# Weight and query loads issued at counted matrix instructions, in a kernel of a delta rule followed by a feed-forward block

## The chip, the cores and the metric

The kernel runs on one core of a Trainium2 chip. The metric is the device time of one execution in microseconds (us). A core has TensorE (PE in the profile, with its weight loads as PEld), VectorE (DVE), ScalarE (ACT), GpSimd (POOL) and SyncE (SP), each with its own queue of instructions in program order. Here SP only issues DMA transfers; they run on 16 shared DMA engines. The same engines also bring in the engines' own code.

## The reference

For each of 4 x 8 heads, over 768 tokens of 48 numbers, a state matrix is carried along by the delta rule; the result, seen as 3072 tokens of 384 numbers, goes through a feed-forward block.

```python
k_n = k / (norm(k) + 1e-6)
for t in range(S):
    y[t] = q[t] @ state
    state = state + beta[t] * outer(k_n[t], v[t] - state.T @ k_n[t])
x = y.transpose(0, 2, 1, 3).reshape(3072, 384)
h = x @ w_in                     # 384 x 2048, 64-bit input
out = (h * sigmoid(h)) @ w_out   # 2048 x 384, 64-bit input
```

## The kernel before

**Tiling.** The 768 tokens are worked through in 6 chunks of 128 (index c), each in two halves of 64 tokens. Inside a chunk the delta rule is solved with triangular matrices: scores of keys with keys and with queries (`score`, L517), the inverse of small 32 x 32 blocks on VectorE (`invert_first` for chunk 0, L653 to L684; `invert` for the others, L606), the joining of the blocks into 64 x 64 (`joins(0)` and `joins(1)`, whose products are L705, L721, L734 and L794), and the state's products (`keys`, `inner`, `old`, `new`, `update`). The score blocks go out to DRAM and come back in another layout (`block_out`, L564; `block_in`, L570). The feed-forward block takes each half's outputs through `hidden` (L1029, products with `w_in`, then Silu on ScalarE) and through `project` (L1064) or `combine` (L1136), which multiply with `w_out`.

**Weights.** The 64-bit weights are loaded in 16 pieces of 768 KB each, 8 of `w_in` (`fetch_w_in(i)`, L283) and 8 of `w_out` (`fetch_w_out(i)`, L295), and each is made 32-bit by `narrow`: two instructions on ScalarE (L224, L225), two on VectorE (L229, L233), one on GpSimd (L237). Pieces land in rooms that something else uses later: `raw` (a pool of three buffers shared with `gT`), `w_outs`, `spare` (in `sums_of_g`), `sums_of_w`.

**Order.** The order on each engine is written out by hand: `pin` chains every instruction behind the one before it on its engine. Every transfer of SP goes through `in_line`, which chains it behind the last transfer; if `pace` holds an instruction, the transfer also waits for that instruction to finish. `linked(fetch, ...)` puts the last transfer into `pace`, so that the next load waits until the one before it has landed. A string of words drives the long first part from L1496 on: `s` one step of solving chunk 0, `f` one step of narrowing, `r` one half of a `hidden` or `project` step, `j` one product of `joins(1)`, `q` one transpose of chunk 1's queries, `l` the lengths of chunk 1's keys, `b` the first two narrowing instructions of the next piece, `W7`, `w2` and `w3` the loads of those pieces, `v` the values of chunk 1. Loops from L1499 on do the same for chunks 1 to 5.

**Around the change.** `busy(n)` (L336) runs n products of `ident` with a state that is still zero, whose result nothing reads. During the 17 steps of `invert_first` the loop at L1330 runs seven of them, each behind a step of the inversion, and four transposes of chunk 1's keys (`turn`, L488). Ahead of that, SP's queue holds in this order: the four block stores of chunk 0 (four more go through ScalarE's queue), `block_in(0)`, `fetch_w_in(0)`, `load_k(1)`, `fetch_w_in(1)`, `load_v(0)`, and then:

```python
linked(fetch_w_in, 2)
linked(load_q, 1)
fetch_w_in(3)
linked(fetch_w_in, 4)
linked(fetch_w_in, 5)
linked(fetch_w_in, 6)
```

Later `W7`, `w2` and `w3` follow out of the string of words, and `fill` issues `w_out` pieces 0, 1 and 4 to 7 as soon as the narrowing of an earlier piece has freed their rooms. An fp32 product is four PE instructions (two weight loads and two products), a transpose two.

Of the kernel before, what the change touches and what calls it, by code (L numbers as in the profile page):

```python
# [11 lines left out]
U32 = mybir.dt.uint32  # L12
# [7 lines left out]
def kernel(  # L20
# [52 lines left out]
            mybir.DependencyInfo(how, mybir.DependencyReason.DATA), reason="order",  # L73
        )

    pins = {}

    def pin(op):

        engine = op.ins.engine  # L80
        if engine in pins:
            behind(op, pins[engine])
        pins[engine] = op
        return op

    line, pace = [], []
# [17 lines left out]
    def go(steps, n=1):  # L104
        for _ in range(n):
            next(steps, None)

    def together(*parts):
        for _ in zip_longest(*parts):
            pass  # L110
# [52 lines left out]
    def in_blocks(c):  # L163

        return 1 < c < NCH
# [3 lines left out]
    def linked(fetch, *args):  # L169

        pace.append(line[-1])
        fetch(*args)

    def load_k(c, bs=ALL):
# [98 lines left out]

    def fetch_w_in(i):
        if i in (0, 1, 6):
            raw = mlp.tile([P, SIZE], U32, name="raw", tag="gT", bufs=3)[:]
        elif i < 6:
            raw = room(i // 2 - 1, i % 2)
        else:
            raw = spare  # L280
        raw = raw.rearrange("p (a f) -> p a f", a=NKT)
        src = moe_w_in.rearrange("(a p) f -> p a f", p=P)[:, :, i * WF : (i + 1) * WF].bitcast(U32)
        in_line(nc.sync.dma_start(out=raw, in_=src))  # L283
        raws["in", i] = raw.rearrange("p a (f j) -> p a f j", j=2)
# [47 lines left out]
    def busy(n=1, after=None, how=NoSync):  # L332

        for _ in range(n):
            pw = bank(CC, "pw")
            done = pin(nc.tensor.matmul(  # L336
                pw[:, 0:DM], lhsT=ident[:],
                rhs=states[0][:].rearrange("p u a w -> p (u a w)")[:, 0:DM], start=True, stop=True,
            ))
            if after is not None:  # L340
                behind(done, after, how)
                after = None
# [138 lines left out]
    def turn(c, b, j, room, by_vector=False):  # L481

        if j == 0:
            kq_room(c, b)
        src, kq = (kbufs[c % 2], queries[c] if c < 2 else None)[j][:, b], kqs[c, b]
        pt = bank(room, "pt")
        for p in range(NP):
            pin(nc.tensor.transpose(  # L488
                pt[:, p * C : (p + 1) * C], src[:, p].rearrange("p e w -> p (e w)"), ident[:]
            ))  # L490
        ptv = pt[:].rearrange("p (a t) -> p a t", a=NP)
        if j == 1:
            if by_vector:
                pin(nc.vector.tensor_scalar(
                    out=kq[:, :, j, :], in0=ptv, scalar1=-1.0, scalar2=None, op0=ALU.mult
                ))
            else:
                pin(nc.scalar.mul(kq[:, :, j, :], ptv, -1.0))
        elif by_vector:
            pin(nc.vector.tensor_copy(out=kq[:, :, j, :], in_=ptv))  # L500
        else:
            pin(nc.scalar.copy(kq[:, :, j, :], ptv))
# [65 lines left out]
    def block_in(c):  # L568
        there, g, _ = blocks[c]
        in_line(nc.sync.dma_start(out=g, in_=there[:]))  # L570
# [716 lines left out]
    def first_queries(b):  # L1287
# [4 lines left out]
        turn(0, b, 1, M)  # L1292
        score(0, b, (1,), (A, CC), evacuate)

    block_in(0)
    busy(4)
    for _ in norm_steps(0):
# [4 lines left out]
    for t in xis:  # L1302
        pin(nc.gpsimd.memset(t, 0.0))
    step = block_steps(0)
    fetch_w_in(0)
    load_k(1)
    fetch_w_in(1)
    load_v(0)
    for c in range(1, NCH):
        beta_of(c)  # L1310
# [1 line left out]
    for b in range(2, B):  # L1312
        first_queries(b)
        busy(1)
    linked(fetch_w_in, 2)
    linked(load_q, 1)
    fetch_w_in(3)
    linked(fetch_w_in, 4)
    linked(fetch_w_in, 5)
    linked(fetch_w_in, 6)  # L1320
    begin(("in", 0))
    inv = invert_first(step)

# [5 lines left out]

    for n in range(1 + Q):  # L1330
        done = next(inv)
        if n in (4, 6, 8, 9, 11, 13, 15):
            busy(1, done, Sync)
        if n in (10, 12, 14, 15):
            turn(1, (10, 12, 14, 15).index(n), 0, M)
    corner, turned, straight = next(inv)
    pin(nc.gpsimd.memset(slab, 0.0))

    def joins(hf, between=()):

        for stage in (
            corner(0, hf), corner(1, hf), turned(0, hf), turned(1, hf), straight(0, hf), merge_half(0, hf, False),
            straight(1, hf), merge_half(1, hf, False), merge_half(0, hf, True), merge_half(1, hf, True),
        ):
            yield from stage
            for what in between[:1]:
                what()
            between = between[1:]

    def filled(n):  # L1350
        return lambda: fill(n)
# [5 lines left out]
    def none():  # L1357
        pass

    together(joins(0, [sized, none, none, filled(2), filled(1), none, none, filled(2), begin_next, none]))  # L1360
    masks(1, 0)
    masks(1, 1)

# [6 lines left out]
    def run(n=1):  # L1370

        for _ in range(n):
            name = next(needed, None)
            if name is not None:
                until(name)
            go(pieces)
            begin_soon()
# [62 lines left out]
    sizes_1 = [0, 1]  # L1440
    sums_made = sum_w()
    later = {}

    def script(text):

        nonlocal pieces
        for word in text.split():
            what, n = word[0], int(word[1:] or 1)
            if what == "s":
                go(solving, n)  # L1450
            elif what == "f":
                fill(n)
                begin_soon()
            elif what == "r":
                run(n)
            elif what == "e":
                eager.append(True)
            elif what == "l":
                go(long, n)
            elif what == "j":  # L1460
                go(rest, n)
            elif what == "q":
                turn(1, queries_1.pop(0), 1, M)
            elif what == "b":
                begin_next()
            elif what == "p":
                go(ready, n)
            elif what == "w":
                fetch_w_out(n)
            elif what == "W":  # L1470
                fetch_w_in(n)
            elif what == "h":
                size_half(1, pins[seen_on])
            elif what == "v":
                load_v(1)
            elif what == "k":
                load_k(2)
            elif what == "g":
                step = block_steps(1)
                pin(nc.gpsimd.memset(spread[:], 0.0))  # L1480
                later["inv"] = invert(1, step)
            elif what == "i":
                go(later["inv"], n)
            elif what == "z":
                size(1, sizes_1.pop(0))
            elif what == "t":
                until(("out", NWI - 1))
                go(sums_made, n)
            elif what == "m":
                go(long_2, n)  # L1490
            elif what == "c":
                run(999)
                pieces = chained(feed_forward(1, 0), feed_forward(1, 1))

    for text in (
        "s f3 s q s q b j20 j8 r j16 f j16 q f j20 r j4 f j32 j8 b j4 q j4 W7 r f r j16 j6 f j4 j8 f j8 f b j8 f j4 j8 r j12 e r f j99 h w2 f r l f s f l r2 w3 l p r l f p l s l f r l r l3 p l s l3 p l2 r l f l4 f l f l3 p l s l2 s2 f r v f r p l3 g i p f l p f i p f l i r3 i r i2 r3 i2 r i r i3 b r2 f2 r3 i r i2 r2 i f b i4 f r f r2 f r3 f i2 r f i f r3 f r f i f r i2 r i2 k i2 b r2 i r i r z r i r s r b z s b r2 t r2 f s r2 t2 m2 t2 b m f r m s f b r m r m2 b m f s r s m4 c s m7 r t s m r m5 s r m m t t",  # L1496
    ):
        script(text)
    for c in range(1, NCH):  # L1499
        if c > 1:  # L1500
            solving = solve(c)
            for n in range(9):
                go(solving)
                run((2, 2, 2, 2, 1, 1, 2, 2, 2)[n])
                if n == 5:
                    pieces = chained(pieces, feed_forward(c, 0), feed_forward(c, 1))
        assert next(solving, 0) == 0
        go(long_2, 99)
        if c + 1 < NCH:
            ready = prepare(c + 1)  # L1510
            go(ready)
            run(2)
            step = block_steps(c + 1)
            for _ in ready:
                run(2)
            run(6)
            for n, _ in enumerate(invert(c + 1, step)):
                run(int(n % 4 != 3 and n != 24))
                if n == 3:
                    load_k(c + 2)  # L1520
                    if in_blocks(c + 2):
                        load_blocks(k, c + 2, ALL)
            after = lengths(c + 2) if c + 2 < NCH else iter(())
            for _ in range(8 if c == 1 else 10):
                run()
                go(after, 4)
            go(after, 99)
    run(999)


# [28 lines left out]
```

## Time and profile before

| what | value |
|---|---|
| three runs | 650.11, 657.17, 660.95 us; median 657.17 |
| the profiled execution | 652.37 us, with a span of 650.4 us from first to last instruction |
| busy share of the span | PE 96%, DVE 61%, ACT 33%, POOL 14% |
| granted clock of TensorE | 0.99 on average; 0.51 from 40 to 50 us |
| DMA | 54.70 MB, mean 84 GB/s |
| PE busy, 20 to 70 us | 41.7 of 50 us |
| PE busy, 200 to 500 us | 300 of 300 us |

Busy shares are means over stages with different limits. The first 100 us hold the start of the delta rule, the loading and narrowing of the weights and the first hidden products; from 200 us on PE is busy without a break. A wait named "issue" is time in which an engine stood still and nothing that the profile shows released it. Queue q1 holds SP's transfers, q10 ScalarE's, q8 and q14 the engines' code.

### The profile page before, as it was taken

To read this page: it belongs to the slowest core of one execution; us is meant where nothing else is said; L and a number is where in the kernel's file an instruction comes from. 1 tells how busy PE (TensorE), PEld (TensorE's weight loads), DVE (VectorE), ACT (ScalarE), POOL (GpSimd) and SP (SyncE) were. 2 spreads that over 40 slices of the span, in tenths; PEclk is the share of its full clock that TensorE was granted. 3 is DMA by queue.
4 is the path that set the end of the run, shared out by engine and by line. 5 is a ranking of instruction groups with operands and counts; after the bars stand their busy time and mean duration, and the time that the engine had idled before them with its cause. 6 is when DMAs were issued, how large, how long until landed. Compare 5 with 4: busy or idle time off the path is not lost.

```text
span 650.4 us, 21395 instructions
## 1 busy us (share of the span) xinstructions
PE 627.6 (96%) x9416; PEld 548.0 (84%) x9416; DVE 397.6 (61%) x911; ACT 213.8 (33%) x497; POOL 90.9 (14%) x92
## 2 busy tenths in 40 slices
PE   7878899999989999999999999999999999999997
PEld 5577778756779989989989989989989989889997
DVE  5875689997764987453986453987454974103112
ACT  2455663332342122451122452122451122451111
POOL 5023631334101020010020010020011000000000
PEclk9979999999989999999999999999999999999999
DMA  9876534250288324268324268324173024100101
GB/s 136 209 165 206 192 75 104 98 97 3 53 154 148 58 73 60 50 136 143 59 76 57 48 131 146 61 74 60 28 153 72 10 65 60 40 13 1 25 0 25
DMA packets 145676, 54.70 MB, mean 84 GB/s; under 512 B 117152, under 2 KB 138912, under 8 KB 145584
## 3 DMA queue, kind: packets, MB, share of 16 engines
q1 hardware_dynamic: 143136, 52.93, 39.6%
q8 instruction: 74, 1.21, 0.8%
q10 hardware_dynamic: 2448, 0.41, 0.4%
q14 instruction: 18, 0.15, 0.1%
HBM read 40.14 MB, written 11.01 MB: 79 GB/s over the span
## 4 chain that ended last, share of the span: by engine, by line
PE 91%; DMA 2%; issue 2%; DVE 2%; ACT 1%; SPq 1%; DVEq 0%
PE phid L1029 38%; PE px L1136 16%; PE py L1136 12%; PE po L1064 5%; PE pb_c L828 3%; PE pa L517 2%; PE pb_c L816 2%; PE pyc L907 2%; PE pb_c L1064 2%; PE pb_c L848 1%; PE pb_c L336 1%; PE pyc L894 1%; DMA kb<-in_k_dram 1%; PE pt L488 1%; PE py L770 1%
## 5 line engine op out<-in xcount | busy, mean ns | idle before, releaser
L1029 PE MATMUL phid<-xT,w_in 128*128 128x256 f32 x1152 | 260.1, 383 | 2.1 <-DMA xT<-part 2.0
L1029 PEld LDWEIGHTS phid<-xT,w_in 128*128 128x128 f32 x1152 | 216.9, 191 | 34.4 <-issue 3.0
L1039 ACT ACTIVATE gT<-phid 128x512 f32<-128x512 f32 x88 | 52.5, 597 | 149.8 <-PE phid L1029 145.2
L615 DVE SCALAR_TENSOR_TENSOR rank<-g,step,x 128x31 f32<-128x31 f32 (+15 forms) x124 | 49.8, 401 | 35.8 <-DMA g<-blocks 32.3
L1118 DVE TENSOR_TENSOR sums_of_g<-gT 128x384 f32<-128x384 f32 (+1 forms) x60 | 29.9, 518 | 59.0 <-ACT gT L1039 48.4
L1136 PE MATMUL py<-w_out,sums_of_g 128*128 128x192 f32 x320 | 56.8, 329 | 0.0
L1136 PE MATMUL px<-sums_of_w,sums_of_g 128*128 128x192 f32 x320 | 56.8, 329 | 0.0
L1136 PEld LDWEIGHTS px<-sums_of_w,sums_of_g 128*128 128x128 f32 x320 | 52.2, 190 | 0.5
L1136 PEld LDWEIGHTS py<-w_out,sums_of_g 128*128 128x128 f32 x320 | 52.2, 190 | 0.4
L620 DVE TENSOR_TENSOR x<-x,rank 128x31 f32<-128x31 f32 (+15 forms) x124 | 42.5, 343 | 4.3
L455 POOL TENSOR_TENSOR vf<-vf,n_slot 128x768 f32<-128x768 f32 x10 | 15.0, 1516 | 169.3 <-DMA vf<-in_v_dram 125.3
L476 DVE STREAM_TRANSPOSE kq<-stage 128x512 f32<-128x512 f32 x28 | 28.5, 1114 | 12.0 <-DMA stage<-in_q_dram 10.4
L532 ACT COPY xT<-pyc 48x128 f32<-48x128 f32 (+2 forms) x126 | 32.6, 259 | 1.6
L1136 PE MATMUL px<-sums_of_w,gT 128*128 128x192 f32 x160 | 28.4, 329 | 0.0
L1136 PE MATMUL py<-w_out,gT 128*128 128x192 f32 x160 | 28.4, 329 | 0.0
L1136 PE MATMUL px<-w_out,gT 128*128 128x192 f32 x160 | 28.0, 327 | 0.0
L1136 PEld LDWEIGHTS px<-w_out,gT 128*128 128x128 f32 x160 | 26.4, 190 | 0.5
L538 POOL COPY g<-x 64x256 f32<-64x256 f32 x4 | 5.0, 1241 | 154.5 <-DVE x L623 154.5
L1136 PEld LDWEIGHTS py<-w_out,gT 128*128 128x128 f32 x160 | 26.1, 190 | 0.3
L1136 PEld LDWEIGHTS px<-sums_of_w,gT 128*128 128x128 f32 x160 | 26.1, 190 | 0.2
L828 PEld LDWEIGHTS pb_c<-vf,xi 64*64 64x64 f32 x736 | 23.5, 138 | 3.2 <-issue 2.9
L1147 DVE TENSOR_TENSOR o<-o,kept 128x192 f32<-128x192 f32 (+1 forms) x29 | 11.5, 422 | 24.0 <-ACT kept L1144 24.0
(221 smaller groups left out, 921.6 us busy)
## 6 DMA issues: line engine op xcount, KB each, us to landing
vf<-in_v_dram SPq DMA_DIRECT2D x48, 96.0 KB, 3.2
out_dram<-o SPq DMA_DIRECT2D x42, 96.0 KB, 2.2
w_out<-in_moe_w_in_dram SPq DMA_DIRECT2D x4, 768.0 KB, 4.4
sums_of_w<-in_moe_w_out_dram SPq DMA_DIRECT2D x4, 768.0 KB, 5.9
blocks<-ap SPq DMA_DIRECT2D x44, 64.0 KB, 1.9
g<-blocks SPq DMA_DIRECT2D x5, 512.0 KB, 3.5
kb<-in_k_dram SPq DMA_DIRECT2D x12, 192.0 KB, 5.1
kb<-in_k_dram SPq DMA_DIRECT2D x24, 96.0 KB, 4.6
```

Source lines behind the costliest of these rows:

```text
L455: pin(nc.gpsimd.tensor_tensor(out=vf, in0=vf, in1=of, op=ALU.mult))
L476: pin(nc.vector.transpose(out=kqs[c, b][:, :, j, :].rearrange("p a (i m) -> p a m i", i=T), in_=src.rearrange("p a (m d) -> p a m d", d=D) ...
L517: pin(nc.tensor.matmul(pa[e][half, p * n * W : (p + 1) * n * W], lhsT=kq[rows, p, 0, half], rhs=kq[rows, p, js[0] : js[-1] + 1, half], sta ...
L532: return pin(nc.scalar.copy(to, of))
L615: pin(nc.vector.scalar_tensor_tensor(out=tv, in0=g[:, 0:m, m : m + 1].to_broadcast([P, m, n]), scalar=step[:, m : m + 1], in1=x[:, m : m + ...
L620: yield pin(nc.vector.tensor_tensor(out=x[:, 0:m, m:T], in0=x[:, 0:m, m:T], in1=tv, op=ALU.add))
L828: yield pin(nc.tensor.matmul(pz[rows, n * D : (n + 1) * D], lhsT=xis[g][rows, u * H + 2 * p + e, :], rhs=vfs[c][rows, hf, g * HB + u, p, : ...
L1029: pin(nc.tensor.matmul(ph[:, j * GT : (j + 1) * GT], lhsT=w_in[:, a, (2 * f + j) * P : (2 * f + j + 1) * P], rhs=xTs[c, hf][:, a, :], star ...
L1039: pin(nc.scalar.activation(out=hidden_of(c, hf, f), in_=ph[:], func=ACTF.Silu, scale=-0.5 if in_blocks(c) else 0.5))
L1064: pin(nc.tensor.matmul(pos[i][:, 0:DM], lhsT=hidden_of(0, hf, f // 2)[:, at : at + C], rhs=w_outs[f // HFF][:, f % HFF, :], start=(f == 0) ...
L1118: pin(nc.vector.tensor_tensor(out=sums_of_g[:, k, fs], in0=of[0], in1=of[1], op=op))
L1136: pin(nc.tensor.matmul(to, lhsT=at, rhs=quarter(f, *b) if isinstance(b, tuple) else sums_of_w[b][:, f], start=start and f == 0, stop=f == ...
```

## The change

A counter in `pin` follows PE's instructions (2 for a transpose, 4 for a product). A list `loads` holds pairs of a count and a load; when the counter reaches a count, `paced` puts the newest PE instruction into `pace` and issues the load, so that SP waits for that instruction. Ten loads are in the list: pieces 2 to 7 of `w_in`, the queries of chunk 1 in two halves, pieces 2 and 3 of `w_out`. `fetch_w_in(0)` goes ahead of `block_in(0)`. The loop around `invert_first` runs two products of `busy` in place of seven. The string of words has some words moved and `W7`, `w2` and `w3` gone; the loops for chunks 1 to 5 are written out as strings of words.

```diff
@@ pin
+        if engine in tensor[:1]:
+            begun[0] += 2 if op.ins.is_transpose else 4
+            while loads and begun[0] >= loads[0][0]:
+                paced(*loads.popleft()[1:])
@@
+    def paced(fetch, *args):
+        pace.append(pins[tensor[0]])
+        fetch(*args)
@@ start of chunk 0
+    fetch_w_in(0)
     block_in(0)
     busy(4)
...
     step = block_steps(0)
-    fetch_w_in(0)
     load_k(1)
-    fetch_w_in(1)
+    paced(fetch_w_in, 1)
     load_v(0)
...
-    linked(fetch_w_in, 2)
-    linked(load_q, 1)
-    fetch_w_in(3)
-    linked(fetch_w_in, 4)
-    linked(fetch_w_in, 5)
-    linked(fetch_w_in, 6)
+    PACKET, WINDOW = 256, 445
+    loads.extend((
+        (WINDOW + PACKET * 2 + 15, fetch_w_in, 2),
+        (WINDOW + PACKET * 3 + 90, fetch_w_in, 3),
+        (WINDOW + PACKET * 4 + 30, load_q, 1, slice(HB * 0, HB * 0 + HB)),
+        (WINDOW + PACKET * 5 + 0, load_q, 1, slice(HB * 1, HB * 1 + HB)),
+        (WINDOW + PACKET * 6 + -15, fetch_w_in, 4),
+        (WINDOW + PACKET * 7 + -15, fetch_w_in, 5),
+        (WINDOW + PACKET * 8 + -15, fetch_w_in, 6),
+        (WINDOW + PACKET * 9 + -15, fetch_w_in, 7),
+        (WINDOW + PACKET * 10 + -15, fetch_w_out, 2),
+        (WINDOW + PACKET * 11 + -75, fetch_w_out, 3),
+    ))
+    raw_6 = mlp.tile([P, SIZE], U32, name="raw", tag="gT", bufs=3)
@@ around invert_first
-        if n in (4, 6, 8, 9, 11, 13, 15):
+        if n == 8:
             busy(1, done, Sync)
-        if n in (10, 12, 14, 15):
-            turn(1, (10, 12, 14, 15).index(n), 0, M)
+        if n == 10:
+            turn(1, 0, 0, M)
+        if n == 12:
+            turn(1, 1, 0, M)
+        if n == 14:
+            turn(1, 2, 0, M)
+        if n == 15:
+            busy(1, done, Sync)
+            turn(1, 3, 0, M)
@@ joins(0): one step of narrowing one place earlier, one begin_next one place earlier
@@ string of words, its beginning
-        "s f3 s q s q b j20 j8 r j16 f j16 q f j20 r j4 f j32 j8 b j4 q j4 W7 r f r j16 j6 f j4 j8 f j8 f b j8 f j4 j8 r j12 e r f j99 h w2 f r l f s f l r2 w3 l p r ...
+        "s f3 s q q s j4 b j36 r j4 f j16 q f j4 f j16 r j44 b j4 q j4 r f r j22 f j12 f j8 f b j8 f j8 r j16 e r f j99 h f r f2 l s l r l p r ...
@@ chunks 1 to 5: the loops' steps as strings of words, in the same order
...
```

More of the change, by code (lines that the diff above doesn't have):

```diff
@@ L74, in behind @@
         )
-    pins = {}
+    pins, tensor, begun, loads = {}, [], [12], deque()
     def pin(op):
@@ L275, in fetch_w_in @@
         if i in (0, 1, 6):
-            raw = mlp.tile([P, SIZE], U32, name="raw", tag="gT", bufs=3)[:]
+            raw = (raw_6 if i == 6 else mlp.tile([P, SIZE], U32, name="raw", tag="gT", bufs=3))[:]
         elif i < 6:
@@ L339, in busy @@
             ))
+            tensor.append(done.ins.engine)
             if after is not None:
@@ L1358, in none @@
         pass
-    together(joins(0, [sized, none, none, filled(2), filled(1), none, none, filled(2), begin_next, none]))
+    together(joins(0, [
+        lambda: (size_half(0, pins[seen_on]), begin_next(),),
+        lambda: (),
+        lambda: (),
+        lambda: (fill(1), fill(1),),
+        lambda: (fill(1),),
+        lambda: (),
+        lambda: (fill(1),),
+        lambda: (fill(1), begin_next(),),
+        lambda: (),
+        lambda: (),
+    ]))
     masks(1, 0)
@@ L1442 @@
     later = {}
+    chunks = {
[5 rows of a table added]
+    }
     def script(text):
@@ L1468, in script @@
             elif what == "w":
-                fetch_w_out(n)
+                paced(fetch_w_out, n)
             elif what == "W":
-                fetch_w_in(n)
+                paced(fetch_w_in, n)
+            elif what == "Q":
+                paced(load_q, 1)
+            elif what == "o":
+                busy(n)
             elif what == "h":
@@ L1495 @@
     for text in (
-        "s f3 s q s q b j20 j8 r j16 f j16 q f j20 r j4 f j32 j8 b j4 q j4 W7 r f r j16 j6 f j4 j8 f j8 f b j8 f j4 j8 r j12 e r f j99 h w2 f r l f s f l r2 w3 l p r l f p l s l f r l r l3 p l s l3 p l2 r l f l4 f l f l3 p l s l2 s2 f r v f r p l3 g i p f l p f i p f l i r3 i r i2 r3 i2 r i r i3 b r2 f2 r3 i r i2 r2 i f b i4 f r f r2 f r3 f i2 r f i f r3 f r f i f r i2 r i2 k i2 b r2 i r i r z r i r s r b z s b r2 t r2 f s r2 t2 m2 t2 b m f r m s f b r m r m2 b m f s r s m4 c s m7 r t s m r m5 s r m m t t",
+        "s f3 s q q s j4 b j36 r j4 f j16 q f j4 f j16 r j44 b j4 q j4 r f r j22 f j12 f j8 f b j8 f j8 r j16 e r f j99 h f r f2 l s l r l p r l f p l s l2 f r3 l3 p l s l3 p l2 r l f l4 f l f l3 p l s l2 s2 f r f r p l3 g i p l p f i p f l i r3 i r v f i2 r3 i2 r i r i3 b r2 f2 r2 i r2 i2 r2 i f b i r i3 f2 r2 f r3 f i2 r f i f r3 f r f i f r i2 r i2 k i2 b r2 i r i r z r i r s r b z s b r2 t r2 f s r2 t2 m2 t2 b m f r m s f b r m r m2 b m f s r s m4 c s m7 r t s m r m5 s r m2 t2",
     ):
@@ L1499 @@
     for c in range(1, NCH):
+        after = lengths(c + 2) if c + 2 < NCH else iter(())
         if c > 1:
             solving = solve(c)
[L1502 to L1506, printed above, removed]
-        assert next(solving, 0) == 0
[L1508 to L1527, printed above, removed]
+            pieces = chained(pieces, feed_forward(c, 0), feed_forward(c, 1))
+        ready = prepare(c + 1)
+        for word in chunks[c].split():
+            what, n = word[0], int(word[1:] or 1)
+            if what == "s":
+                go(solving, n)
+            elif what == "r":
+                run(n)
+            elif what == "y":
+                go(ready, n)
+            elif what == "g":
+                step = block_steps(c + 1)
+                inverse = invert(c + 1, step)
+            elif what == "i":
+                go(inverse, n)
+            elif what == "k":
+                load_k(c + 2)
+                if in_blocks(c + 2):
+                    load_blocks(k, c + 2, ALL)
+            elif what == "m":
+                go(after, n)
+            elif what == "l":
+                go(long_2, n)
+        assert next(solving, 0) == 0
     run(999)
```

5 rows, old and new, of the table chunks are left out of this document.

## The prediction

> **What bounds the kernel now.** I read the page first, then the windows by stage, then what TensorE (PE) waited for, the chain of waits and the queue of the SP engine, and last the DMA record beside the count of PE's instructions.
>
> ```profile
> span 650.4 us, 21395 instructions
> PE 627.6 (96%) x9416; PEld 548.0 (84%) x9416; DVE 397.6 (61%) x911; ACT 213.8 (33%) x497; POOL 90.9 (14%) x92
> ...
> q8 instruction: 74, 1.21, 0.8%
> ```
>
> PE is the bound. From 194 us to the end it is busy 451.6 of 456 us; nothing that the change touches lies there, and the strings of words for chunks 1 to 5 spell out the same steps as the loops did. All that can move lies before 194 us, above all between 20 and 70. The last line is the kernel's own code arriving: 1.21 MB in 74 packets is 16.4 KB each, and PE's 2 x 9416 instructions over 74 packets make 254 for each. What PE waited for between 30 and 70 us is only this:
>
> ```profile
> PE pl L734 <- issue: 2.6, 2, 1.4
> PE pb_c L794 <- issue: 1.9, 1, 1.9
> PE py L794 <- issue: 1.7, 1, 1.7
> PE pl L721 <- issue: 0.5, 1, 0.5
> ```
>
> "issue" is time with no releaser. I counted PE's instructions up to each of these five gaps: 1200, 1455, 2215, 2471, 2726. They are 255 or 256 apart, or three times that: PE has run to the end of a packet of code and the next has not come. The windows show why four of the five last so long (busy us of each engine, granted clock, DMA share, GB/s):
>
> ```profile
> 50.20:53.60 3.40, 3.30 (x115) 2.77 (x114) 1.01 (x2) 2.99 (x5) 1.45 (x1) 1.00 0.73 231
> 53.60:54.65 1.05, 1.05 (x67) 0.80 (x66) 0.51 (x2) 0.35 (x1) 0.00 (x0) 1.00 0.06 16
> ...
> 55.20:58.15 2.95, 2.42 (x54) 1.83 (x55) 2.83 (x5) 0.60 (x1) 1.84 (x1) 1.00 0.77 261
> 58.15:59.20 1.05, 1.05 (x93) 1.01 (x90) 0.63 (x2) 1.03 (x4) 0.00 (x0) 1.00 0.08 23
> 59.20:60.50 1.30, 0.06 (x7) 0.00 (x0) 1.13 (x3) 1.30 (x3) 0.00 (x0) 1.00 0.39 50
> ```
>
> A weight load fills the DMA engines until 53.6 and 58.2; in the microsecond behind it little moves but one packet of code (16 GB/s for 1.05 us is 16.8 KB), and PE stands still from 59.26 to 60.50. In the DMA record the packets of code start at 39.97, 53.63, 58.19 and 64.89; the 768 KB loads ahead of them end at 40.06, 53.63 and 58.40, and the two loads of 1.5 MB ahead of the last end mainly at 64.8. The fetch gets its turn when the load has drained. Third, the clock:
>
> ```profile
> 39.64:49.88 10.24, 8.38 (x211) 8.11 (x212) 7.62 (x14) 4.86 (x11) 1.97 (x2) 0.50 0.76 168
> ```
>
> For 10.24 us PE had half its clock, just after a stretch (36.2 to 39.6) with a gap of 1.38 us and otherwise only 32-row products.
>
> **The change, part by part.**
>
> *Loads at counted instructions.* A packet is asked for when PE crosses into the packet before it. Where nothing was in the way, the fetch starts 1.05 (68.40 after 67.35), 0.78, 0.77 and 1.21 us after the crossing, 0.95 on average. From its start until PE goes on takes 2.62, 2.40, 2.32, 2.31 and 2.46 us in the five gaps, 2.42 on average. So a packet used up in less than 3.4 us makes a gap, even undisturbed. The four disturbed fetches started 1.71, 1.91, 2.24 and 4.39 us after their crossings (38.26, 51.72, 55.95, 60.50): 0.76, 0.96, 1.29 and 3.44 late. What each can give back is the smaller of lateness and gap: 0.76 of 1.86, all of 0.53, of 1.25 and of 1.67, together **4.2 us**. The gap of 1.38 at 36.88 stays: its fetch was on time (35.64 after 34.52) and its packet lasted 2.2 us.
>
> The new loads must not collide in their turn. The counter of the diff stands some 8 above my count, so the loads wait for instructions 964, 1295, 1491, 1717, 1958, 2214, 2470, 2726, 2982 and 3178, most of them at a crossing. Data came 1.04 us after SP's issue (36.13 to 37.17) and lasted 2.9 to 3.3 us, so a load fills about 1.3 to 4.4 us after its crossing, behind the fetch at 0.95. It is clear of the next one if the packet lasts 3.4 us: with today's gaps taken out they last 3.5 (1967 to 2215), 3.1, 5.0 and 6.4 us. The load of piece 3 is put 95 instructions past its crossing, where packets last 2.0 us, and falls into the slow stretch. I count no new gap. No weight comes late: ScalarE (ACT) begins pieces 2 to 7 at 43.8, 52.2, 59.2, 65.4, 72.4 and 74.1, and their loads are issued near 34.9, 38.8, 51.7, 55.2, 58.5 and 63.5 with 4.4 us to landing. The last has the least room: 67.9 against 74.1 - 4.2 = 69.9; before, it was issued at 59.35. The first half of the queries, issued near 42.7 over 1.9 us and 3.8 to 4.7 to landing, comes at 48 to 49, and the first product on it ran at 49.36: hidden, by little.
>
> What waits behind a load on SP: it is first in, first out, so whatever the program issues after a load waits until PE reaches its count. Those are later loads, the pieces of w_out freed by narrowing, and the block stores (from 80.6), which follow in PE's order anyhow. Nothing for this.
>
> *Five products left out.* Each costs PE 0.65 us (10 instructions in 3.42 us at 26.3), 3.2 us in all. They ran back to back with four transposes and made PE late: the first joining product (L705) started at 33.37, and its operand was ready at 32.25. But its reader waits on VectorE (DVE):
>
> ```profile
> 32.10 1.93 DVE L682 STREAM_TRANSPOSE sums_of_w<-sums_of_w 128x1024 f32<-128x1024 f32 x1
> 34.12 0.34 DVE L712 SCALAR_TENSOR_TENSOR sums_of_w<-pl,second,pick 64x128 f32<-64x128 f32 x1
> ```
>
> DVE is busy until 34.03, so only 34.12 - 34.03 is won: **0.1 us**. If that transpose were not there, it would be 1.1.
>
> *First weights ahead of the blocks' return.* SP ends its block stores at 14.38 and waits until 17.21 to issue the return; DVE begins on it at 20.71, which is 17.21 plus the median landing of 3.5, so every delay goes straight into the inversion. The load now issued in that wait moves 768 KB from about 15.5. Below: nothing, if it is through by 18.2, when the return's data began. Above: a whole load, 2.9 us, if the return queues behind all of it. The block packets of both queues run until 16.1, so I expect the load to end near 18.8 and take **0.6 us**. Its earlier landing wins nothing: ACT takes up that piece at 26.91 and had its data at 22.6. The second piece's wait for PE is over (20.2) before SP reaches it.
>
> *Moved words* (query transposes, two runs of hidden products, one fill, the load of the next values): the same instructions in another order, none on a wait listed above. Zero, with 0.5 either way.
>
> **Sum**: 650.4 - 4.2 - 0.1 + 0.6 = 646.7 us of span, and 1.97 around it (652.37 - 650.4): **648.7 us**. The profiled execution is a low one: the three runs are 650.1, 657.2 and 661.0, so the median stands 4.8 above my base.
>
> [...]
>
> **The rivals.**
>
> *The half clock goes too.* It began after the stretch with the 1.38 us gap. In it 43 instructions of L872 took 1.31 us, and 48 just after it 0.86: a ratio of 0.59. PE works from 42.37 to 49.88 nearly without a gap, so 7.5 x 0.41 = 3.1 us more, and with the blocks' return free 652.4 - 4.2 - 0.1 - 3.1 = **645.0**. For it: the gaps after 38 us shorten. Against: the joining products themselves stay as small.
>
> *Nothing changes.* Gaps would come from PE using packets up too fast, load or no load. For: the 1.38 gap had no late fetch. Against: four fetches that started as a load ended. 652.4 + 0.6 = **653.0**.
>
> *Slower: the loads get in ahead of the fetch.* Load and fetch are both set off at the crossing, 1.3 and 0.95 us before their data. If the load is first, the fetch starts at about 4.2 and the packet is usable at 6.6 us. Packets that last 2.2, 2.0, 3.5, 3.1 and 5.0 us then leave gaps of 4.4, 4.6, 3.1, 3.5 and 1.6: 17.2 in place of today's 6.7. 652.4 + 10.5 = **662.9**. It decides as soon as the margin of 0.35 us is gone. Against it: undisturbed fetches never took over 1.21 us.
>
> *The clock falls for longer.* From 26 to 33 us PE would do about 2 us of full products and 1.8 of transposes in place of 6.9. A second stretch of 10.24 us at half clock, over dense products, costs 5.1: **653.8**. Against: the windows from 5.5 on were 70% busy and kept their clock. [...]
>
> **How the numbers follow.** Forecast 0.40; half clock gone too 0.28; loads ahead of the fetch 0.14; longer half clock 0.10; nothing 0.08. The prediction is 648.7. Runs of one kernel lie 11 us apart here, so 2% (13 us) is about what a measurement can tell from no change. The low end, 640, is the second case less half that spread; the high end, 662, reaches the slower rival and takes in a whole load ahead of the blocks (651.0) and the upper half of the runs. Against the median of 657.2, over 2% faster means under 644.0: half of the second case and a third of the forecast, 0.28. Over 2% slower means above 670: a good part of the slower rival's upper half and a little of the clock's, 0.10. The rest is 0.62.
>
> **What would show it.** Right: packets of code start about 1 us after each crossing between 38 and 70 us; of the five gaps, those near 36.9 and 40.5 remain at 1.1 to 1.4 and the others are gone; L656 starts at 20.7 to 21.5; L712 starts when L682 ends. Wrong: gaps of over 2 us on "issue", a fetch that starts as a counted load ends, L656 after 22, a second row at clock 0.5 before 100 us, or a new wait of PE on a weight or on the queries near 49.

## The result

The changed kernel takes 649.26 us in the median of 22 runs (646.9 to 651.73), the kernel before 652.74 us (22 runs, 649.48 to 661.08). The ratio is 0.9947, 95% interval 0.9925 to 0.9970: faster by about 3.5 us, within 2%. The profiled execution took 648.18 us with a span of 646.2 us. The forecast was 648.7 us, a saving of 3.7 us on the profiled execution, which fell by 4.2. The forecast took the profiled execution of before (652.37 us) as its base and not the median of three runs, 657.17; the 22 runs, with a median of 652.74, bear that choice out.

The page of the changed kernel, the lines that answer to those shown of before:

```profile
span 646.2 us, 21378 instructions
...
PE 624.3 (97%) x9406; PEld 546.1 (85%) x9406; DVE 398.0 (62%) x911; ACT 214.3 (33%) x497; POOL 91.0 (14%) x92
...
PE 76%; DVE 11%; DMA 7%; SPq 2%; issue 2%; ACT 1%; ACTq 0%; POOL 0%; DVEq 0%; POOLq 0%
```

PE is busy for 3.3 us less, about what the five products took (5 x 0.65 us), and the chain that ended last (last line) no longer runs over PE alone: it was PE 91%, DVE 2% and DMA 2%. We come back to that. What PE waited for between 30 and 70 us (line numbers are 10 higher behind the inserted lines):

```profile
PE pb_c L345 <- DVE sums_of_w L678: 1.3, 1, 1.3
PE px L804 <- issue: 1.0, 1, 1.0
PE pl L715 <- DVE sums_of_w L688: 0.7, 1, 0.7
PE pl L731 <- issue: 0.7, 1, 0.7
PE py L804 <- issue: 0.5, 1, 0.5
...
```

The three gaps on issue that are left lie in the joining stage, before 43 us; those of before near 55, 59 and 66 us are gone. PE crosses into new packets of code at 51.63, 55.54, 59.30, 63.63 and 69.99 us, and in the DMA record the next packets start at 52.40, 56.43, 59.92, 64.55 and 70.62, 0.6 to 0.9 us later; before, it was 1.9 to 4.4 us for the three behind the gaps at 55, 59 and 66. In the joining two fetches still start as a counted load ends: at 40.51 and 44.28, 1.3 and 1.5 us after their crossings, with loads that end at 40.60 and 44.40. The windows by stage (from the third number on: PE, PEld, DVE, ACT, POOL, then the granted clock):

```profile
35.99:49.64 13.65, 12.14 (x431) 11.69 (x432) 10.44 (x20) 6.45 (x15) 4.21 (x3) 0.50 0.53 150
50.00:60.00 10.00, 9.63 (x340) 7.93 (x339) 6.22 (x14) 6.36 (x12) 3.72 (x2) 1.00 0.68 196
60.00:70.00 10.00, 10.00 (x249) 8.01 (x251) 7.24 (x12) 7.91 (x16) 4.94 (x3) 1.00 0.70 214
```

PE was busy 8.63 and 7.82 us in the last two stretches before and is now at 9.63 and 10.00. The half clock did not go: it starts 3.65 us earlier and lasts 13.65 us instead of 10.24. The start of the inversion moved from 20.71 to:

```profile
22.05 0.69 DVE L666 TENSOR_TENSOR sums_of_w<-sums_of_w,step 128x512 f32<-128x512 f32 x1 [2.25 <-DMA sums_of_w<-blocks]
```

Following the same VectorE, ScalarE and GpSimd instructions through both traces gives a ledger of how far the changed kernel is ahead (minus) or behind:

| at (time of before) | difference, us | what lies before it |
|---|---|---|
| 26 to 29 | +1.35 | blocks' return behind the first weights |
| 46 | +0.18 | shorter code gaps in the joining |
| 59 | -0.59 | |
| 72 | -3.87 | gaps at 55, 59 and 66 gone |
| 100 to 148 | -3.9 | |
| 151 | -5.46 | gap at 149.7 gone |
| 201 | -7.08 | wait at 186.4 shorter (0.51 for 1.66), half clock from 189.8 to 193.2 gone |
| 255 | -5.89 | new waits at 240.3 and 245.5 |
| 350 | -4.40 | new wait at 338.9 |
| end | -4.20 | |

### The profile page after: what moved, and what is told of

The parts are those of the page before. It is cut to its first block, busy times and chain, and to the rows that moved or that the text cites. A ratio compares the mean times of both kernels' runs of the same rounds, so it can differ in the third digit from the quotient of the medians.

```text
span 646.2 us, 21378 instructions
## 1 busy us (share of the span) xinstructions
PE 624.3 (97%) x9406; PEld 546.1 (85%) x9406; DVE 398.0 (62%) x911; ACT 214.3 (33%) x497; POOL 91.0 (14%) x92
## 3 DMA queue, kind: packets, MB, share of 16 engines
q8 instruction: 74, 1.21, 0.8%
## 4 chain that ended last, share of the span: by engine, by line
PE 76%; DVE 11%; DMA 7%; SPq 2%; issue 2%; ACT 1%; ACTq 0%; POOL 0%; DVEq 0%; POOLq 0%
PE phid L1039 30%; PE px L1146 13%; PE py L1146 10%; PE po L1074 5%; DVE rank L625 4%; DVE x L630 3%; PE pb_c L838 3%; PE pa L527 2%; PE pb_c L826 2%; PE pb_c L1074 2%; PE pyc L917 1%; PE pb_c L858 1%; DMA up<-x 1%; DVE sums_of_g L1128 1%; PE pyc L904 1%
## 5 line engine op out<-in xcount | busy, mean ns | idle before, releaser
L625 DVE SCALAR_TENSOR_TENSOR rank<-g,step,x 128x31 f32<-128x31 f32 (+15 forms) x124 | 49.7, 401 | 37.5 <-DMA g<-blocks 34.1
L838 PEld LDWEIGHTS pb_c<-vf,xi 64*64 64x64 f32 x736 | 23.5, 138 | 4.0 <-issue 3.7
```

What stands on the lines that cost most here:

```text
L625: pin(nc.vector.scalar_tensor_tensor(out=tv, in0=g[:, 0:m, m : m + 1].to_broadcast([P, m, n]), scalar=step[:, m : m + 1], in1=x[:, m : m + ...
L838: yield pin(nc.tensor.matmul(pz[rows, n * D : (n + 1) * D], lhsT=xis[g][rows, u * H + 2 * p + e, :], rhs=vfs[c][rows, hf, g * HB + u, p, : ...
```

## The experiments

The theory: a fetch of code waits until the load ahead of it has drained; the counted loads give each fetch its turn, and this carries the gain; the blocks' return costs about 1 us; the products cost nothing; what PE saves before 200 us is partly given back to the inversions of chunks 2 and 3, which become the limit. Rivals: the five products carry the gain; the clock does; the places of the loads do not matter. Every ratio is to runs of the kernel before on the same chip, with its 95% interval; the changed kernel's is 0.9947 (0.9925 to 0.9970).

**Parts undone or done alone.** First the order of the first weights and the blocks' return:

```diff
-    fetch_w_in(0)
     block_in(0)
...
     step = block_steps(0)
+    fetch_w_in(0)
     load_k(1)
```

> The changed kernel, with the first weights behind the blocks' return again. If the load ahead of the return is what makes the inversion of chunk 0 start at 22.06 us in place of 20.71, L656 starts at 20.7 here, the joining products start about 1.3 us earlier than in the changed kernel, and the time is 0.5 to 1.4 us below it (less than 1.3 if a later wait takes some back), about 648. Rival: the joining stage is bound by the arrival of code, 3.4 us for each packet, so the 1.3 us are lost again by 43 us and the time stays at 649.

Ratio 0.9921 (0.9898 to 0.9943), 648.5 us. The inversion starts at 21.01:

```profile
21.01 0.69 DVE L666 TENSOR_TENSOR sums_of_w<-sums_of_w,step 128x512 f32<-128x512 f32 x1 [1.05 <-DMA sums_of_w<-blocks]
```

Over all profiles of this study it starts at 20.64 to 21.40 in the seven kernels with the return first (mean 20.9) and at 21.71 to 22.48 in the six with the weights first (mean 21.9). The order costs the inversion 1.0 us; in the end 1.7 us (0.26%) against the changed kernel, but the two intervals overlap.

Then the seven products back, in the changed kernel, with the four transposes at their old places:

```diff
-        if n == 8:
+        if n in (4, 6, 8, 9, 11, 13, 15):
             busy(1, done, Sync)
```

> The changed kernel, with all seven unread products and the old places of the four transposes. If the products hide behind the inversion, the time stays within 0.7 us of the changed kernel (649) and L712 starts when L682 ends. Rival, products on the path: 5 x 0.65 = 3.2 us slower, 652. Rival, the clock: the products keep the clock up, so the half clock begins one window of 3.4 us later than at 36.0 us, and the time is about 1 us lower.

Ratio 0.9959 (0.9930 to 0.9988), 0.8 us above the changed kernel, less than the intervals can separate. The half clock starts at 39.33 and lasts 10.24 us, as before the change: without the five products it comes 3.34 us earlier, at 35.99, as the clock rival had it, but that did not make the kernel with products faster.

With both edits together, only the counted loads and the moved words of the change are left:

> The kernel before with the counted loads and the moved words alone: the first weights behind the blocks' return, seven unread products. If the counted loads carry the whole gain, the gaps on issue near 55, 59 and 66 us are gone and the time is 1 us or so below the changed kernel, 648, so 4 to 5 us below the kernel before. Rival, the gain comes from the products: 652 to 653, as before.

Ratio 0.9962 (0.9935 to 0.9989). PE's waits between 30 and 60 us:

```profile
PE pb_c L804 <- issue: 1.6, 1, 1.6
PE pl L744 <- issue: 1.2, 1, 1.2
PE pb_c L838 <- issue: 1.2, 1, 1.2
...
```

The gaps near 55, 59 and 66 us are gone here too, and from 48 to 71 us this kernel wins 4.3 us on the kernel before (from +1.07 to -3.20), as the changed one does (4.1). The time was expected 4 to 5 us below before and is 2.5 below. In its profile it stands 5.97 us ahead of the kernel before at 201 us and 1.82 at the end: it gives back more than the changed kernel does (7.08 and 4.20). So the counted loads, with the moved words, account for most of the gain; the intervals cannot say whether for all.

And the products alone, in the kernel before (the loop of the changed kernel around `invert_first`, nothing else):

> The kernel before with five of the seven unread products left out and nothing else changed. If they hide behind the inversion: no change, within 0.7 us of the kernel before (652.7). Rival, products on the path: 3.2 us faster, 649.5. Rival, the clock: the half clock begins earlier, or lasts longer, by one or two windows of 3.4 us; up to 3 us slower.

Ratio 0.9996 (0.9970 to 1.0022). Left out by themselves they win nothing in time. Where the prediction looked for their price, its reading holds: L712 starts at 33.97 us in place of 34.12. But the joining behind it then loses more to late code:

```profile
PE px L794 <- issue: 3.6, 1, 3.6
PE py L794 <- issue: 2.4, 1, 2.4
```

In the kernel before, these two gaps are 1.9 and 1.4. The fetch after the crossing at 39.20 starts at 42.85, as a load ends at 42.85. So the ratio alone does not say whether the products were hidden, or saved something that late code took back (this profile is also 2.3 us above the median of its runs). Beside the counted loads they seem to win: 0.9921 without five of them against 0.9962 with all, both with the return first. The last part comes back to this.

**The places of the loads.** All ten counts raised by half a packet:

```diff
-        (WINDOW + PACKET * 2 + 15, fetch_w_in, 2),
+        (WINDOW + PACKET * 2 + 143, fetch_w_in, 2),
... (the other nine also by 128)
```

> The changed kernel with all ten counts raised by 128 instructions, half a packet of code. If a fetch waits for the load ahead of it, a load set off half a packet (1.5 to 2.5 us) later fills the engines until 6 to 7 us after the crossing, past the next one, and fetches start 2 to 3 us after their crossings instead of 0.6 to 0.9: gaps on issue of 0.5 to 2 us come back between 50 and 66 us, and the time rises by 2 to 4 us over the changed kernel, to 651 to 653. Rival, it is enough that each load waits for something and that they do not pile up: no gaps, 649. Rival, weights that come late: new waits on narrowing, not on issue.

Ratio 1.0089 (1.0064 to 1.0114): about 9 us slower than the changed kernel, far more than expected. The fetches did what the theory says: after the crossings at 63.06, 67.70, 72.04 and 85.56 they start at 65.47, 69.55, 75.58 and 89.09, 1.9 to 3.5 us later, and the loads end at 65.73, 69.82, 75.58 and 89.09. But few gaps were expected in the right place. PE's waits, 30 to 70 us:

```profile
PE pt L498 <- DMA sums_of_g<-in_q_dram: 2.3, 1, 2.3
PE py L804 <- issue: 2.2, 1, 2.2
PE px L804 <- issue: 0.9, 1, 0.9
PE pb_c L804 <- issue: 0.7, 1, 0.7
PE pl L731 <- issue: 0.6, 1, 0.6
```

The 2.2 us at L804 come with a load in the joining; between 50 and 66 us packets lasted over 5 us and the late fetches mostly did no harm. The queries, set off half a packet later, cost 2.3 us at once: the room of 1 us that the prediction gave them is real. The clock was also at half for 34.1 us in that profile, in four stretches (from 21.3, 41.8, 55.4 and 86.1 us), in place of 13.65. Because of the queries and the clock this run does not tell the places apart; all counts lowered by 80 does, as the queries then come earlier:

```diff
-    PACKET, WINDOW = 256, 445
+    PACKET, WINDOW = 256, 365
```

> The changed kernel with all ten counts lowered by 80 instructions, so that a load fills the engines from about the crossing on and not from 1.3 us after it. If a fetch waits for whatever load is ahead of it, fetches start when the load ends, 3 to 4 us after their crossings instead of 0.6 to 0.9, gaps on issue of 0.5 to 2.5 us come back between 38 and 70 us, and the time rises by 3 to 6 us, to 652 to 655. Rival, half a packet later was slow only because the queries came late: no gaps and 649, since the queries come earlier here.

Ratio 0.9992 (0.9966 to 1.0018): some 3 us slower than the changed kernel, so the whole gain is gone; the two intervals just touch (0.9966 and 0.9970). Its waits and windows:

```profile
PE py L804 <- issue: 2.7, 1, 2.7
PE pl L731 <- issue: 2.1, 2, 1.8
...
```

```profile
35.75:38.55 2.80, 2.68 (x130) 2.55 (x131) 1.92 (x5) 0.82 (x3) 2.26 (x2) 0.50 0.88 271
38.55:39.50 0.95, 0.00 (x0) 0.00 (x0) 0.91 (x3) 0.63 (x2) 0.00 (x0) 0.50 0.14 45
39.50:41.09 1.59, 0.00 (x0) 0.00 (x0) 1.12 (x2) 0.00 (x0) 0.31 (x1) 0.50 0.00 0
```

The crossing is at 35.69, the load moves 271 GB/s until 38.55, then a packet of code and hardly anything else moves, and PE stands still from 38.43 to 41.09 with the DMA engines empty for the last 1.6 us. In the changed kernel the same gap is 0.48. Likewise the fetch after the crossing at 54.01 starts at 57.06, as a load ends at 57.24, and PE stands still for 1.81 us from 57.62. Followed through both profiles, this kernel falls 5.6 us behind the changed one between 37 and 66 us, the stretch of these gaps, and little elsewhere; part of that stretch also lies at half clock (33.6 to 50.7 and 60.9 to 64.3 us). A shift of 80 instructions with the same transfers loses what the change won: it is the place that counts. This is the third rival of the prediction, brought about by the edit. The prediction put it 10.5 us above the kernel before; it came out level with that kernel, since two large gaps opened and not five.

**What is given back after 200 us.** Every second rank step of the inversions of chunks 2 to 5 is left out, in the changed kernel and in the kernel before (the inverse is then incomplete, and only the time is of use):

```diff
         for m in range(T - 1, 0, -1):
+            if c > 1 and m % 2 == 0:
+                yield
+                continue
```

> The changed kernel, which leaves out every second rank step of the inversions of chunks 2 to 5 (15 of 31 steps, some 11 us of VectorE in each chunk). If the saving up to 200 us (7.1 us in the profiles) is partly given back because TensorE then waits for the inversion of chunks 2 and 3, those waits (py <- xe near 240 and 339 us) are gone and the time falls by 2 to 3 us, to about 646.5. Rival, nothing is given back there and the difference after 200 us is the clock alone: 649, as the changed kernel.

> The kernel before with the same steps left out. TensorE had no wait between 200 and 500 us there, so the time stays within 0.7 us of the kernel before. Then the two short kernels differ by 6 to 7 us where the full ones differ by 3.5. If it falls by as much as the changed one, the inversion was no special limit of the changed kernel.

The changed kernel falls to 0.9902 (0.9879 to 0.9925), the kernel before stays at 1.0001 (0.9969 to 1.0032). The short pair is 1.0% apart, 6.5 us; the full pair 0.5%, 3.5 us. In the short changed kernel PE waits for nothing from 230 to 350 us. So about 3 us of what the change saves before 200 us are given back because the inversion of chunks 2 and 3 then comes last. The two intervals of the changed kernel, full and short, only touch at 0.9925; it is the pair of short kernels that separates clearly. The chain of the changed kernel shows by what path:

```profile
229.88 1.24 DVE x L633
...
231.23 1.26 POOL g L548
232.50 0.46 SPq L106
233.00 4.05 DMA up<-x
237.12 0.31 SPq L648
...
237.79 2.78 DMA xe<-low
240.61 0.39 PE py L780 x24
```

Two trips through DRAM, 4.05 and 2.78 us, lie between the last step on VectorE and the first product that needs it. In the kernel before, the chain from 229 to 247 us was one row of hidden products:

```profile
228.88 18.35 PE phid L1029 x85
```

**The clock.** Five unread products between the joining stages of chunk 0 in the changed kernel (`lambda: ()` becomes `lambda: busy(1)` five times):

> The changed kernel with five unread products put between the joining stages of chunk 0 (after stages 2, 3, 6, 9 and 10). If the half clock from 36.0 to 49.6 us comes from too little work in a window of the joining, it begins later or is shorter by one or two windows, and the time falls by 1 to 3 us. Rival: the joining is bound by code and by its readers, so five products of 0.65 us and 20 more instructions cost 1 to 3 us and the half clock stays.

Ratio 1.0015 (0.9990 to 1.0041): slower by 4 to 5 us than the changed kernel. In the profile the half clock begins 5 us later and is as long as before:

```profile
41.16:54.81 13.65, 13.65 (x285) 10.61 (x284) 7.72 (x15) 5.28 (x11) 2.76 (x2) 0.50 0.51 110
```

The clock does not explain the loss. The profile, with one more stretch at half clock from 20.7 to 27.5 us, is the run with the lowest mean clock of the twelve (0.981). One run had the full clock throughout (1.000) and took 654.36 us against the median of 654.63, and the five with 0.994 or more lie between 651.42 and 657.12. No run of any other kernel here has a mean clock above 0.992, so the products did keep the clock up in some runs, and won nothing by it. The loss comes in the joining: followed through both profiles, this kernel is 0.3 us behind the changed one at 40 us, 4.0 at 48 and 4.6 from 52 to 80; its first hidden product runs at 57.31, behind the stretch at half clock.

Other kernels follow the clock from run to run in part. Of 27 runs of the kernel before on one chip, the three with a mean clock of 0.982 or less took 659.3 to 660.7 us and the six with 0.990 or more 651.2 to 655.1; of 23 on another chip, the three at 0.981 or less took 658.0 to 658.7 and the two at 0.990 654.0 and 659.0; for the changed kernel it is 650.5 us on average over the seven runs at 0.984 or less and 648.8 over the others. Where in a run that extra half clock lay is not known without a profile.

**The products once more.** Seven products again, five of them 32 columns wide, with the return first:

```diff
-            busy(1, done, Sync)
+            busy(1, done, Sync, DM if n in (8, 15) else T)
```

> The changed kernel with the first weights behind the blocks' return, and seven unread products, five of them only 32 columns wide: the same code as with loads alone, but nearly none of TensorE's 3.2 us. With loads alone the time was 651.6, with five products left out it was 648.5. If TensorE's time was the cost, this one stays at 648.5, the joining starts at 32.6 us. If it was the 20 instructions of code (where the packets of code end in the joining stage), it is back at 651 to 652. Rival, both are the spread of the runs: anything between, with intervals that overlap.

And all seven left out, with the return first:

> The changed kernel with the first weights behind the blocks' return and all seven products of that loop left out. If they only cost, the time falls by up to 1 us below 648.5. Rival, the clock: with four transposes as the only work of TensorE from 26 to 32 us, the half clock begins one or two windows of 3.4 us earlier, and the time rises by 1 to 3 us.

The narrow ones came to 0.9940 (0.9914 to 0.9966), between the two it was to tell apart; both intervals reach it, so nothing is decided. One more thing parts the kernels with counted loads and seven products around the inversion, wide or narrow, from those with two or none: in their three profiles PE also stands still for 1.1 us at the start of L838. That gap lies 141 instructions behind a crossing, so it is no late code; ScalarE's copies of `xi`, which L838 reads, stand there behind two narrowing instructions (43.11 to 44.87 in the run with seven wide products) and start at 44.90. Narrow products have it as well, so it does not come from the time that the products take on TensorE. None at all: 0.9893 (0.9854 to 0.9931), 649.35 against 652.42 us for the narrow ones on the same chip. In that kernel the half clock begins at 33.25 and lasts longest:

```profile
33.25:50.32 17.07, 13.35 (x546) 12.71 (x537) 11.84 (x23) 6.44 (x15) 4.68 (x3) 0.50 0.53 136
```

and yet this kernel has the lowest ratio of all kernels that do the whole work, 1.1% below the kernel before. It would be the version to take, though it ran six times only and its interval just overlaps that of the changed kernel.

## Why the prediction came out right, step by step

- **A fetch waits for the load ahead of it, and the counted loads free it.** Right in mechanism, place and size: 3.45 us were forecast for the three gaps behind 48 us, and the ledger shows 4.1 between 46 and 72. The earlier 0.76 in the joining cannot be read alone, since the half clock moved there. The two runs with shifted counts show the cause: with the same transfers at other places, fetches again start as loads end.
- **The gaps that were to stay** near 36.9 and 40.5 at 1.1 to 1.4 us became 0.48 and 1.00, and one of 0.69 at 34.94 is new, so this was wrong in size. Work that took 2.36 and 2.26 us between gaps before (34.52 to 36.88, 38.26 to 40.52) takes 3.14 and 2.57 at the half clock that now starts ahead of it: the packets lasted 0.78 and 0.31 us longer, and their successors came less late.
- **Five products: 0.1 us.** Alone they are worth nothing in time (0.9996), and L712, which the prediction named as the limit, moves by 0.15 us. With the counted loads, kernels without them were faster in both pairs, by 0.1% and 0.4%, the intervals of the second pair barely overlapping. Whether that is TensorE's time or the 20 instructions of code, which move every gap of the joining, stays open: the run with narrow products lies in between, and its gap at L838 speaks for the code. The profiles of the second pair stand 5.97 (with) and 5.73 us (without) ahead of before at 201 us and 1.82 and 2.70 at the end, so what parts these two profiles is not won around the products.
- **Blocks' return: 0.6 us.** The right sign, too small: 1.35 us in this pair of profiles, 1.0 on average over thirteen. The load ahead of it ran until 19.2 us, not 18.8, and the last of the blocks landed behind it: the return took 4.5 us to land in place of 3.5, and was issued at 17.50 in place of 17.21. Two of the signs that the prediction had put down for being wrong came true in small: this start behind 22 us, and the two fetches in the joining that start as counted loads end.
- **Moved words: zero.** Not tested by themselves.
- **What was not foreseen** nearly cancels, by luck: 3.2 us won between 100 and 200 us (a code gap, a wait at 186 and the short half clock after it) and 2.9 us given back after 240. The prediction wrote that nothing after 194 us would be touched; the short kernels show that the saving itself touched it, by making the inversions the limit. The win between 100 and 200 us is also not in every profile: the run with seven products stands 2.3 us ahead of before at 148 and 2.1 at 201. So the path up to 72 us was forecast by its mechanism, and the fit of the total within about 0.5 us is in part luck.
- **The rivals.** "Nothing changes" falls by the run with counts 80 lower. "The half clock goes too" was wrong, "the clock falls for longer" right in what the clock did (13.65 us for 10.24, 17.07 with no products at all) and wrong in its price: in the joining PE is held up by code and by its readers, and the run with no half clock at all among the twelve with products in the joining was no faster (654.36 us against a median of 654.63). With fewer products around the inversion the half clock of the joining started earlier: at 39.33 us with seven, 35.99 with two and 33.25 with none, and in the kernel before with five left out at 37.4 for 13.65 us in place of 39.6 for 10.24. It also started at 33.6 with two products and the counts 80 lower, so the number of products is not all of it. By what rule the clock falls was not shown.

## What to carry to other kernels

Look at the count of instructions at gaps with no releaser: in the kernel before the five lay 255 or 256 apart, or three times that, and at each the next packet of code had not come. Then look at the place of large loads against the crossings. In the changed kernel the data of three 768 KB loads began 1.25, 1.31 and 1.32 us after the crossings at 51.63, 55.54 and 59.30, and the fetches had their turn ahead of them, 0.6 to 0.9 us after the crossing; the same loads 80 instructions earlier took the whole gain away (0.9992 for 0.9947). After a saving on the busiest engine, follow one instruction stream through both traces to the end: what is won early can be given back where another chain comes last, here the inversion with its two trips through DRAM.

## What the runs showed of the hardware

In these traces a fetch of 16 KiB of code is on a queue of its own (q8) and yet, with a 768 KB load under way, started as the load ended, within about 0.3 us in the cases told here: at 39.97, 53.63 and 58.19 us before, with loads that end at 40.06, 53.63 and 58.40, and at 40.51 and 44.28 in the changed kernel, with 40.60 and 44.40. The DMA engines were not idle at every start: in the kernel before, where several loads followed one another, a fetch started at 64.89 us, and from 64.85 to 65.90 the engines moved 393 GB/s. With nothing in its way a fetch started 0.77 to 1.21 us after the crossing in the kernel before, and with no load under way 0.62 to 0.92 in the changed one, at 52.40, 56.43, 59.92 and 64.55. At the gaps PE went on 2.31 to 2.62 us after the start of the fetch in the kernel before, and 2.32 to 3.10 in the changed one. From the averages in the kernel before, 0.95 and 2.42, an estimate follows: a packet that lasts less than about 3.4 us would make PE wait even with the DMA engines empty.

Half clock came in stretches of 3.41 us (the kernel before, from 189.8), 6.83 (products in the joining, from 20.7), 10.24 (before, from 39.64), 13.65 (the changed kernel, from 35.99) and 17.07 (no products, from 33.25), multiples of 3.41. In three profiles (later counts, products in the joining, narrow products: from 21.3, 20.7 and 20.7 us) it came at a place where no other had it. In the first two nothing ahead of that place had been edited: with the same instructions ahead of it, the changed kernel kept its full clock there.
